# A gated layer with two weight blocks readied early and multiplied side by side, and its first halves paced 4:8

## The chip, the cores and the metric

One core of a Trainium2 chip runs the whole program in one launch. The metric is the device time of that execution in microseconds (us); lower is better. Three executions of the kernel before were timed on the chip, and one more was recorded by the hardware profiler.

## The reference

Four sequences of 448 positions pass through three layers one after the other. All inputs are float32.

```python
# attention: 4 batches x 12 heads, 448 x 64 per head
scores = cap * tanh((q @ k.T / 8) / cap)
attn = exp(scores - max); attn = attn / (sum(attn) + 1e-9)
x = attn @ v                               # [4, 448, 768]
# gated layer: 768 -> 1024 -> 768
h = maximum(x @ w_in, 0)
conv = 3-tap convolution of h along the sequence, per channel (conv_w)
x = (h * (1 / (1 + exp(-conv)))) @ w_out
# mixing: tokens (448 -> 256 -> 448), then channels (768 -> 1536 -> 768), each with a residual
u  = x + (maximum(x.T @ w_tok1, 0) @ w_tok2).T
out = u + maximum(u @ w_ch1, 0) @ w_ch2
```

## The kernel before, in words

Each operand of a product is kept as a high and a low part of a shorter type, and each product is three matmuls (`split3`: high by high, high by low, low by high). A matmul is mostly 128 x 128 weights on 128 x 448 data.

**Attention** is walked through in 96 iterations (`gi`), four to a pair of heads. An iteration multiplies scores (L146, L147), ACT makes them exponentials (L168, L169), DVE splits those into `ah` and `al` (L175, L176), and later PE multiplies them by the values (L195 to L197).

**The gated layer** of batch b is the generator `gated(b)`. Its first half has MF = 8 blocks of 18 matmuls (L466, weights `wi`). After each block ACT and DVE make one pair `gh`, `gl` out of it by Relu, convolution and gate (L470, L475 to L481); the pair of block 7 is ready last. The second half has KD = 6 blocks of 24 matmuls (L492): block m takes the weights `wo` of block m and all eight pairs, in the order k = 0 to 7, three matmuls each. So the last three matmuls of a block need pair 7. ACT takes the block's sum out of PSUM (L496), SP stores it (L497). The tiles `wo` have two buffers.

**The weights wo** are wider numbers in the input and have to be narrowed. For b = 0, `load_wo` does that in three parts of each block: 384 columns (k = 0 to 2), 384 (k = 3 to 5) and 256 (k = 6 and 7). A part is loaded by SP into `w_raw` (L352), ACT and DVE work on it in `w_pt` (L354, L357 to L359), ACT writes the high part of `wo` (L362) and DVE the low part (L366), and SP stores both to `wo_d` (L427). `w_raw` and `w_pt` have one buffer each, which other weights use too. For b over 0 a block comes back from `wo_d` by a single load of 1,024 KB (L435).

**What sets the order.** The generators are interleaved with attention by numbers of units: each `yield` says how many units the piece before it counts (W_IN in the first half, W_OUT in the second), and every iteration of attention draws 11.5 to 13 units (RATES). gated(0) to gated(2) run inside the attention of batches 1 to 3, and gated(3) beside the first steps of token mixing (L701 transposes, L718 and L732 products). Each half is 24 pieces, so the layer is 24 x 5 + 24 x 7 = 288 units. The scheduler orders each engine's instructions by priorities that follow from the place in the program; each engine, and SP's queue of DMAs, runs its own list in order.

Of the kernel before, what the change touches and what calls it, by code (L numbers as in the profile page):

```python
# [9 lines left out]
F32 = mybir.dt.float32  # L10
F32R = mybir.dt.float32r
U32 = mybir.dt.uint32
AF = mybir.ActivationFunctionType
# [4 lines left out]
B, H, S, D = 4, 12, 448, 64  # L18
NP = H // 2
DM = H * D  # L20
KD = DM // 128
DFF = 1024
MF = DFF // 128
# [7 lines left out]
QK = S + KW  # L31
YTB = 9
TKS = 100
W_IN = 5
W_OUT = 7
O_MAG = 6000
O_CAP = 0
O_SC = 0
# [35 lines left out]
def split3(whi, wlo, xhi, xlo):  # L74
    return ((whi, xhi), (whi, xlo), (wlo, xhi))
# [228 lines left out]
def fused_kernel(ctx, tc, ins, out, attention):  # L304
    nc = tc.nc
# [9 lines left out]
    ps_m = ctx.enter_context(tc.tile_pool(name="ps_m", bufs=2, space=PSUM))  # L315
# [75 lines left out]
    for _ in range(WARM):  # L391
        ps = ps_m.tile([128, 512], F32, name="mm")
# [26 lines left out]
    wo = {}  # L419

    def make_wo(m, lo, hi):

        if lo == 0:
            wo[0, m] = wo_p.tile([128, 2, MF * 128], F32R, name="wo", bufs=2)
        t = wo[0, m][:, :, lo:hi]
        narrow(st_p, 384, wide["w_out"][m, :, 2 * lo : 2 * hi], (t[:, 0], t[:, 1]))
        nc.sync.dma_start(wo_d[m, :, :, lo:hi].bitcast(F32), t.bitcast(F32))  # L427

    def load_wo(b, m):
        if b == 0:  # L430
            for lo in range(0, 1024, 384):
                make_wo(m, lo, min(1024, lo + 384))
            return
        wo[b, m] = wo_p.tile([128, 2, MF * 128], F32R, name="wo", bufs=2)
        nc.sync.dma_start(wo[b, m].bitcast(F32), wo_d[m].bitcast(F32))  # L435
# [22 lines left out]

    def gated(b):
        gs = []  # L460
        for m in range(MF):
            hi, lo = win[m]
            ps = ps_m.tile([128, 512], F32, name="mm")
            for k in range(KD):
                for n, (w, v) in enumerate(split3(hi[:, k], lo[:, k], *X[b, k])):
                    nc.tensor.matmul(ps[:, 0:S], w, v, start=k == 0 and n == 0, stop=k == KD - 1 and n == 2)  # L466
                if k % 2 and k < KD - 1:
                    yield W_IN
            h = hb[m % 2]
            nc.scalar.activation(h[:, 1 : S + 1], ps[:, 0:S], AF.Relu)  # L470
            gh = g_p.tile([128, S], F32R, name="gh", bufs=8)
            gl = g_p.tile([128, S], F32R, name="gl", bufs=8)
            gs.append((gh, gl))
            c = cv_p.tile([128, S], F32, name="c", bufs=4)
            nc.scalar.activation(c, h[:, 1 : S + 1], AF.Copy, scale=cw[:, m, 1:2])  # L475
            nc.vector.scalar_tensor_tensor(out=c, in0=h[:, 0:S], scalar=cw[:, m, 0:1], in1=c, op0=ALU.mult, op1=ALU.add)
            nc.vector.scalar_tensor_tensor(out=c, in0=h[:, 2 : S + 2], scalar=cw[:, m, 2:3], in1=c, op0=ALU.mult, op1=ALU.add)
            nc.scalar.activation(c, c, AF.Tanh, scale=0.5)
            nc.vector.scalar_tensor_tensor(out=c, in0=c, scalar=1.0, in1=h[:, 1 : S + 1], op0=ALU.add, op1=ALU.mult)
            nc.scalar.copy(gh, c)  # L480
            nc.vector.tensor_tensor(gl, c, gh.bitcast(F32), op=ALU.subtract)  # L481
            yield W_IN
        load_wo(b, 0)
        for m in range(KD):
            if m + 1 < KD:
                load_wo(b, m + 1)
            w = wo.pop((b, m)).rearrange("p t (k n) -> p t k n", n=128)
            hi, lo = w[:, 0], w[:, 1]
            ps = ps_m.tile([128, 512], F32, name="mm")
            for k in range(MF):  # L490
                for n, (w, v) in enumerate(split3(hi[:, k], lo[:, k], *gs[k])):
                    nc.tensor.matmul(ps[:, 0:S], w, v, start=k == 0 and n == 0, stop=k == MF - 1 and n == 2)  # L492
                if k % 2 and k < MF - 1:
                    yield W_OUT
            y = cv_p.tile([128, S], F32, name="c", bufs=4)
            nc.scalar.activation(y, ps[:, 0:S], AF.Copy, scale=0.5)  # L496
            nc.sync.dma_start(y_d[b, m], y)  # L497
            yield W_OUT

    def w2_early(c, i):  # L500

# [22 lines left out]
    for gi in range(NG + 3):  # L524
        g, i = divmod(gi, 4)
# [47 lines left out]
        if gi >= 24 and s3 == 4 and gi < NG:  # L573
            for p in range(NP):
                norm(b3 - 1, p, rr[b3 - 1])
            fills.append(gated(b3 - 1))
# [115 lines left out]
    def tokens(b):  # L692
# [34 lines left out]
        for m in range(KD):  # L727
# [8 lines left out]
            yield 6  # L736

    last = gated(B - 1)
    load_y(0)
    toks = [t for b in range(B - 1) for t in [tokens(b)]]  # L740
# [3 lines left out]
    n = k = 0  # L744
    begun = False
    while True:
        w = next(last, None)
# [276 lines left out]
```

## Time and profile before

| | us |
|---|---|
| median of three timed executions | 903.06 (899.55 to 904.08) |
| the profiled execution, its own time | 902.45 |
| span of that execution in the trace | 900.6 |
| PE busy | 867.5 |
| DVE busy | 696.1 |
| ACT busy | 495.5 |

The profile gives times from the start of the span; 1.85 us of the profiled execution's time lie outside it. The mean granted clock of TensorE over the span is 0.991 of full speed. The first matmul of gated(0) starts at 91.5 us and the first of its second half at 138.7 us; the second half of gated(3) has its last matmul at 522.7 us, and channel mixing takes the rest.

### The profile page before, as it was taken

The page shows a single profiled execution, that of the slowest core. Times are in us where ns is not written, and L with a number is a line of the kernel's source. Part 1 is how long each engine was busy: PE and PEld are TensorE (multiplying, and loading weights), DVE is VectorE, ACT ScalarE, POOL GpSimd, SP SyncE. Part 2 cuts the span into 40 slices and gives each one's busy share as a digit, 9 for nine tenths or more (in the row PEclk, how much of TensorE's full clock was granted, in tenths as well). Part 3 has the DMA queues.
Part 4 walks back from the last instruction along what each step waited for, and adds up shares of the span by engine and source line. Part 5 has one row for each costly group of instructions (what it writes and reads, how often), then busy time and mean ns, then how long its engine had stood idle before and what let it go on. Part 6 is the DMA issues. An engine that isn't in the chain of part 4 may idle for free.

```text
span 900.6 us, 12120 instructions
## 1 busy us (share of the span) xinstructions
PE 867.5 (96%) x4105; PEld 754.4 (84%) x4105; DVE 696.1 (77%) x1271; ACT 495.5 (55%) x820; POOL 4.7 (1%) x19
## 2 busy tenths in 40 slices
PE   8999999989989999999999998999999999999997
PEld 4665887868978889888989988789989899999996
DVE  7889987789997899956897576796967859478342
ACT  6889888767886779863764243442423423143110
POOL 0000000000000000000000000000000000000000
PEclk9999999999999999999999999999999999999999
DMA  7875564667557864457658766556473744517234
GB/s 277 268 219 171 170 201 147 208 210 243 162 177 265 283 219 145 132 181 263 219 162 258 245 199 199 157 176 195 123 245 96 224 151 126 182 55 224 76 109 140
DMA packets 81719, 168.91 MB, mean 188 GB/s; under 512 B 12050, under 2 KB 57586, under 8 KB 79346
## 3 DMA queue, kind: packets, MB, share of 16 engines
q1 hardware_dynamic: 81650, 168.07, 58.1%
q8 instruction: 34, 0.56, 0.3%
q14 instruction: 35, 0.29, 0.1%
HBM read 126.58 MB, written 38.54 MB: 183 GB/s over the span
## 4 chain that ended last, share of the span: by engine, by line
PE 54%; DVE 19%; DMA 15%; ACT 7%; issue 4%; SPq 1%; POOL 0%; DVEq 0%; ACTq 0%; POOLq 0%
PE mm L911 18%; PE o L873 14%; PE mm L492 9%; DMA w_raw<-in_w_in 3%; DMA w_raw<-in_w_out 2%; DMA c<-u_d 2%; PE mm L466 2%; PE ps_e L718 2%; PE ps_e L732 2%; DMA w_d<-w_pt 1%; DVE ab L115 1%; DMA raw<-in_qk 1%; PE ps_s L147 1%; DVE w_pt L358 1%; PE ps_s L146 1%
## 5 line engine op out<-in xcount | busy, mean ns | idle before, releaser
L911 PE MATMUL mm<-hs,w 128*128 128x448 f32 x864 | 178.4, 367 | 0.8 <-DVE rr L912 0.7
L911 PEld LDWEIGHTS mm<-hs,w 128*128 128x128 f32 x864 | 161.7, 188 | 16.2 <-DVE rr L912 1.4
L492 PE MATMUL mm<-gh,wo 128*128 128x448 f32 x384 | 127.1, 374 | 6.4 <-ACT wo L362 3.4
L466 PE MATMUL mm<-xx,wi_h 128*128 128x448 f32 x384 | 114.7, 370 | 0.2 <-DVE xx L453 0.2
L492 PEld LDWEIGHTS mm<-gh,wo 128*128 128x128 f32 x384 | 72.8, 190 | 17.2 <-ACT wo L362 5.4
L146 PE MATMUL ps_s<-ab 128*128 128x448 f32 x192 | 81.6, 426 | 2.9 <-DVE ab L115 2.1
L466 PEld LDWEIGHTS mm<-xx,wi_h 128*128 128x128 f32 x384 | 71.7, 188 | 9.2 <-issue 1.9
L168 ACT ACTIVATE a<-ps_s,icap 128x896 f32<-128x896 f32 x76 | 67.0, 885 | 22.4 <-PE ps_s L147 17.9
L492 PE MATMUL mm<-gl,wo 128*128 128x448 f32 x192 | 71.2, 371 | 0.4 <-DVE gl L481 0.4
L147 PE MATMUL ps_s<-low,ab 128*128 128x448 f32 x192 | 71.3, 373 | 0.3 <-DVE low L116 0.3
L169 ACT ACTIVATE a<-a,cap 128x896 f32<-128x896 f32 x76 | 70.4, 926 | 1.3
L466 PE MATMUL mm<-xx,wi_l 128*128 128x448 f32 x192 | 70.3, 366 | 0.0
L176 DVE TENSOR_TENSOR al<-a,ah 128x896 fp32r<-128x896 f32 (+1 forms) x56 | 54.3, 971 | 1.7
L873 PE MATMUL o<-u,wi_h 128*128 128x448 f32 x216 | 49.4, 363 | 1.4 <-ACT u L790 1.1
L790 ACT CAST u<-c 128x448 fp32r<-128x448 f32 x48 | 27.0, 567 | 42.5 <-DVE c L798 21.9
L873 PE MATMUL o<-u,wi_l 128*128 128x448 f32 x216 | 47.9, 362 | 0.0
L146 PEld LDWEIGHTS ps_s<-ab 128*128 128x128 f32 x192 | 36.3, 190 | 13.4 <-issue 5.0
L175 DVE CAST ah<-a 128x896 fp32r<-128x896 f32 (+1 forms) x56 | 31.5, 565 | 18.9 <-PE ob L196 9.6
L873 PEld LDWEIGHTS o<-u,wi_h 128*128 128x128 f32 x216 | 40.5, 188 | 5.1 <-ACT u L790 1.9
L147 PEld LDWEIGHTS ps_s<-low,ab 128*128 128x128 f32 x192 | 36.4, 190 | 9.0 <-issue 5.4
L873 PEld LDWEIGHTS o<-u,wi_l 128*128 128x128 f32 x216 | 40.5, 187 | 2.7
L111 ACT CAST ab<-raw 128x960 fp32r<-128x960 f32 x36 | 35.4, 992 | 12.3 <-DMA raw<-in_qk 7.1
(166 smaller groups left out, 1690.5 us busy)
## 6 DMA issues: line engine op xcount, KB each, us to landing
wo<-wo_d SPq DMA_DIRECT2D x18, 1024.0 KB
raw<-in_qk SPq DMA_DIRECT2D x18, 960.0 KB
w_raw<-in_w_ch SPq DMA_DIRECT2D x40, 384.0 KB
c<-u_d SPq DMA_DIRECT2D x60, 224.0 KB
w_raw<-in_w_in SPq DMA_DIRECT2D x16, 384.0 KB
e<-in_qk SPq DMA_DIRECT2D x6, 960.0 KB
y_d<-c SPq DMA_DIRECT2D x24, 224.0 KB
yt<-y_d SPq DMA_DIRECT2D x24, 224.0 KB
```

The lines of the kernel that those rows point to most:

```text
L111: nc.scalar.copy(h, r)
L146: nc.tensor.matmul(ps[:, bank, 0:S], a[:, keys], a[:, 0:S], start=start, stop=False)
L147: nc.tensor.matmul(ps[:, bank, 0:S], a[:, keys], low, start=False, stop=stop)
L168: nc.scalar.activation(a[:, 0:n], ps[:, 0:n, 0:S], AF.Tanh, scale=self.c["icap"])
L169: nc.scalar.activation(a[:, 0:n], a[:, 0:n], AF.Exp, scale=self.c["cap"])
L175: nc.vector.tensor_copy(ah[:, 0:n], a[:, 0:n])
L176: nc.vector.tensor_tensor(al[:, 0:n], a[:, 0:n], ah[:, 0:n].bitcast(F32), op=ALU.subtract)
L466: nc.tensor.matmul(ps[:, 0:S], w, v, start=k == 0 and n == 0, stop=k == KD - 1 and n == 2)
L492: nc.tensor.matmul(ps[:, 0:S], w, v, start=k == 0 and n == 0, stop=k == MF - 1 and n == 2)
L790: nc.scalar.copy(w[:, 0], t)
L873: nc.tensor.matmul(ps, l, r, start=k == 0 and n == 0, stop=k == 2 and n == 2)
L911: nc.tensor.matmul(ps[:, 0:S], l, x, start=r == 0 and n == 0, stop=r == 3 and n == 2)
```

## The change

The pieces of gated(0) count 4 units in the first half and 8 in the second in place of 5 and 7 (the sum stays 288); those of the other layers keep 5 and 7. The weights of blocks 0 and 1 are asked for ahead of the blocks m = 5 and m = 7 of the first half, not at its end; those of block m + 2 when block m is done. For b over 0 the second half multiplies block 0 up to k = 6, then block 1 up to k = 6, then k = 7 of block 0 and of block 1, and then blocks 2 to 5 whole. For b = 0 the blocks keep their order.

```diff
-W_IN = 5
-W_OUT = 7
+PACE = (4, 8), (5, 7)
+WO_AT = 5, 7
...
     def gated(b):
         gs = []
+        w_in, w_out = PACE[b > 0]
         for m in range(MF):
+            if m in WO_AT:
+                load_wo(b, WO_AT.index(m))
...
-            yield W_IN
-        load_wo(b, 0)
-        for m in range(KD):
-            if m + 1 < KD:
-                load_wo(b, m + 1)
-            w = wo.pop((b, m)).rearrange("p t (k n) -> p t k n", n=128)
-            hi, lo = w[:, 0], w[:, 1]
-            ps = ps_m.tile([128, 512], F32, name="mm")
-            for k in range(MF):
-                for n, (w, v) in enumerate(split3(hi[:, k], lo[:, k], *gs[k])):
-                    nc.tensor.matmul(ps[:, 0:S], w, v, start=k == 0 and n == 0, stop=k == MF - 1 and n == 2)
-                if k % 2 and k < MF - 1:
-                    yield W_OUT
+            yield w_in
+        acc = {}
+
+        def mm(m, k):
+            if k == 0:
+                acc[m] = ps_m.tile([128, 512], F32, name="mm")
+            w = wo[b, m].rearrange("p t (k n) -> p t k n", n=128)
+            for n, (l, v) in enumerate(split3(w[:, 0, k], w[:, 1, k], *gs[k])):
+                nc.tensor.matmul(acc[m][:, 0:S], l, v, start=k == 0 and n == 0, stop=k == MF - 1 and n == 2)
+
+        def done(m):
+            del wo[b, m]
             y = cv_p.tile([128, S], F32, name="c", bufs=4)
-            nc.scalar.activation(y, ps[:, 0:S], AF.Copy, scale=0.5)
+            nc.scalar.activation(y, acc.pop(m)[:, 0:S], AF.Copy, scale=0.5)
             nc.sync.dma_start(y_d[b, m], y)
-            yield W_OUT
+            if m + 2 < KD:
+                load_wo(b, m + 2)
+
+
+        blocks = [[(0, k) for k in range(MF - 1)] + [(1, k) for k in range(MF - 1)] + [(0, MF - 1), (1, MF - 1)]] if b else [[(m, k) for k in range(MF)] for m in range(2)]
+        blocks += [[(m, k) for k in range(MF)] for m in range(2, KD)]
+        n = 0
+        for m, k in (i for l in blocks for i in l):
+            mm(m, k)
+            if k == MF - 1:
+                done(m)
+            n += 1
+            if n % 2 == 0:
+                yield w_out
```

Line numbers move with it: L466 becomes L469, L475 to L481 become L478 to L484, L492 becomes L493, L496 and L497 become L498 and L499, and every line from L504 on moves by 15.

**First place.** DVE in the first layer, at the `al` of the head whose values PE multiplies at 145.81 us in the trace of before. Before (`c`, `gl` and `h1` are the gate's tiles, `w_pt` the weights being narrowed, `low`, `ab` and `v2` the splitting of queries, keys and values):

```order
L175 CAST ah_1365<-a_1362 128x896 [waits Activation_49]
L476 SCALAR_TENSOR_TENSOR c_1253<-h1_179,cw_94,c_1253 128x448 [waits Activation_49]
L357 TENSOR_SCALAR w_pt_1384<-w_pt_1384 128x384 [waits Activation_49]
L477 SCALAR_TENSOR_TENSOR c_1253<-h1_179,cw_94,c_1253 128x448 [waits DVE_49]
L115 TENSOR_TENSOR ab_1462<-raw_1369,ab_1462 64x512 [waits Activation_49]
L116 TENSOR_TENSOR low_1463<-raw_1369,ab_1462 128x448
L479 SCALAR_TENSOR_TENSOR c_1253<-c_1253,h1_179 128x448 [waits Activation_49]
L358 SCALAR_TENSOR_TENSOR w_pt_1384<-w_raw_1383,w_pt_1384 128x384 [waits DMAHW4_49,DVE_49]
L136 TENSOR_TENSOR v2_1471<-vs_1472,v1_1467 128x512 [waits DMAHW0_49,Activation_49]
L359 SCALAR_TENSOR_TENSOR w_pt_1384<-w_pt_1384 128x384 [waits DVE_49]
L481 TENSOR_TENSOR gl_1252<-c_1253,gh_1251 128x448 [waits Activation_49]
L176 TENSOR_TENSOR al_1366<-a_1362,ah_1365 128x896
```

And now:

```order
L482 SCALAR_TENSOR_TENSOR c_1271<-c_1271,h1_179 128x448 [waits Activation_49]
L175 CAST ah_1418<-a_1415 128x896 [waits Activation_49]
L484 TENSOR_TENSOR gl_1270<-c_1271,gh_1269 128x448 [waits Activation_49]
L176 TENSOR_TENSOR al_1419<-a_1415,ah_1418 128x896 [waits DVE_49]
L357 TENSOR_SCALAR w_pt_1353<-w_pt_1353 128x384 [waits Activation_49]
L115 TENSOR_TENSOR ab_1515<-raw_1422,ab_1515 64x512 [waits Activation_49]
L358 SCALAR_TENSOR_TENSOR w_pt_1353<-w_raw_1352,w_pt_1353 128x384 [waits DMAHW4_49,DVE_49]
```

Between `ah` and the `al` that goes with it stood ten instructions, among them three of narrowing and four of the gate; now one of the gate stands there.

**Second place.** PE in the first layer, in the last block of its second half (number 5), at the last of its weights' three parts (k = 6 and 7). Before, with the end of the 16 rows (18 matmuls) of the next layer's first block that stand between k = 5 and k = 6:

```order
L466 MATMUL mm_2019<-xx_1985,wi_h0_241 128x448 [waits Activation_49]
L466 MATMUL mm_2019<-xx_1985,wi_h0_241 128x448
L466 MATMUL mm_2019<-xx_1985,wi_l0_242 128x448
L466 MATMUL mm_2019<-xx_1991,wi_h0_241 128x448 [waits Activation_49]
L466 MATMUL mm_2019<-xx_1991,wi_h0_241 128x448 [waits DVE_49]
L466 MATMUL mm_2019<-xx_1991,wi_l0_242 128x448
L466 MATMUL mm_2019<-xx_1997,wi_h0_241 128x448 [waits Activation_49]
L466 MATMUL mm_2019<-xx_1997,wi_h0_241 128x448 [waits DVE_49]
L466 MATMUL mm_2019<-xx_1997,wi_l0_242 128x448
L492 MATMUL mm_1878<-gh_1179,wo_1750 128x448 [waits Activation_49]
L492 MATMUL mm_1878<-gl_1180,wo_1750 128x448
L492 MATMUL mm_1878<-gh_1179,wo_1750 128x448 [waits DVE_49]
```

Now, from k = 5 on:

```order
L493 MATMUL mm_1871<-gh_1056,wo_1714 128x448
L493 MATMUL mm_1871<-gh_1137,wo_1714 128x448
L493 MATMUL mm_1871<-gl_1138,wo_1714 128x448
L493 MATMUL mm_1871<-gh_1137,wo_1714 128x448
L451 MATMUL mm_1994<-rr_1924,sel_177 128x448 [waits DVE_49]
L493 MATMUL mm_1871<-gh_1185,wo_1714 128x448 [waits Activation_49]
L493 MATMUL mm_1871<-gl_1186,wo_1714 128x448
L493 MATMUL mm_1871<-gh_1185,wo_1714 128x448 [waits DVE_49]
L493 MATMUL mm_1871<-gh_1269,wo_1714 128x448
L493 MATMUL mm_1871<-gl_1270,wo_1714 128x448
L493 MATMUL mm_1871<-gh_1269,wo_1714 128x448
L469 MATMUL mm_2019<-xx_1967,wi_h0_241 128x448 [waits DVE_49]
```

The next layer's first block (now L469) has moved behind the whole of block 5. From the first matmul of k = 3 of this block to the first of k = 6 there are 13 rows of PE now; between them no row of the next layer is left.

**Third place.** PE in the second layer, at the last pair. Before, in block 0 (`mm_2527`):

```order
L492 MATMUL mm_2527<-gh_2427,wo_2523 128x448 [waits Activation_49]
L492 MATMUL mm_2527<-gl_2428,wo_2523 128x448 [waits DVE_49]
L195 MATMUL oa_2707<-ah_2592,v1_1235 128x448
L492 MATMUL mm_2527<-gh_2427,wo_2523 128x448
L196 MATMUL oa_2707<-ah_2592,v2_2510 64x448
L197 MATMUL oa_2707<-al_2593,v1_1235 128x448 [waits DVE_49]
L492 MATMUL mm_2527<-gh_2483,wo_2523 128x448 [waits Activation_49]
L195 MATMUL oa_2707<-ah_2592,v1_1235 128x448
L196 MATMUL oa_2707<-ah_2592,v2_2510 64x448
L197 MATMUL oa_2707<-al_2593,v1_1235 128x448
L146 MATMUL ps_s_2714<-ab_2505 128x448 [waits PE_49]
L147 MATMUL ps_s_2714<-low_2506,ab_2505 128x448
```

Now block 0 is `mm_2527` and block 1 is `mm_2578`, whose k = 0 to 6 stands ahead of k = 7 of block 0:

```order
L197 MATMUL ob_2730<-al_2679,v1_1333 128x448 [waits DVE_49]
L493 MATMUL mm_2527<-gh_2487,wo_2326 128x448 [waits Activation_49]
L195 MATMUL ob_2730<-ah_2678,v1_1333 128x448
L493 MATMUL mm_2527<-gl_2488,wo_2326 128x448
L196 MATMUL ob_2730<-ah_2678,v2_2514 64x448
L493 MATMUL mm_2527<-gh_2487,wo_2326 128x448
L197 MATMUL ob_2730<-al_2679,v1_1333 128x448
L493 MATMUL mm_2578<-gh_2487,wo_2458 128x448
L493 MATMUL mm_2578<-gl_2488,wo_2458 128x448
L493 MATMUL mm_2578<-gh_2487,wo_2458 128x448
L146 MATMUL ps_s_2795<-ab_2636 128x448 [waits PE_49,Activation_49]
L147 MATMUL ps_s_2795<-low_2637,ab_2636 128x448
```

The pairs 6 and 7 began six rows apart in block 0; now the other block's k = 0 to 6 stands between them, and pair 7 is first used 44 rows later in PE's list. On DVE eight instructions stood between the `ah` and the `al` of the head multiplied here (`al_2593` before); now one does. Block 2 begins 26 rows behind the last row of block 0, and its first row is the one that waits for a DMA, the load of its weights. The same place of the last layer on SP, where that load (`wo_4783`) is issued, now:

```order
L750 DMA u_d_81<-yt_4180 128x448 [waits DVE_49]
L750 DMA u_d_81<-yt_4183 128x448 [waits DMAHW0_49,DVE_49]
L499 DMA y_d_80<-c_4780 128x448 [waits Activation_49]
L435 DMA wo_4783<-wo_d_79 128x2048 [waits DMAHW2_49,PE_49]
L703 DMA yt_4684<-y_d_80 128x448 [waits DMAHW7_49]
L704 DMA yt_4684<-y_d_80 128x64
L703 DMA yt_4687<-y_d_80 128x448 [waits DMAHW5_49,DMAHW0_49]
```

In before, the load of the block behind block 0 stood ahead of the store of block 0 (L497); now it stands behind this store and behind two stores of `u_d`, which wait for DVE.

## Rows read from the trace of the kernel before

**Rows 1.** Page, part 1: busy us, share of the span, instructions

```profile
PE 867.5 (96%) x4105; PEld 754.4 (84%) x4105; DVE 696.1 (77%) x1271; ACT 495.5 (55%) x820; POOL 4.7 (1%) x19
```

**Rows 2.** Windows: stretch, then busy us (count) per engine, clock, DMA

```profile
150.00:175.00 25.00, 25.00 (x124) 22.31 (x123) 18.35 (x34) 17.84 (x29) 0.00 (x0) 0.99 0.53 177
175.00:200.00 25.00, 20.83 (x89) 16.52 (x88) 22.42 (x38) 18.13 (x28) 0.63 (x1) 0.93 0.61 198
```

**Rows 3.** Waits of PE, 138 to 220 us: total us, times, longest

```profile
PE mm L492 <- ACT wo L362: 3.4, 3, 1.4
```

**Rows 4.** PE, timeline of first layer: start, us, instruction, [idle before <-releaser]

```profile
145.81 0.47 PE L197 MATMUL oa<-al,v 128*128 128x448 f32 x1 [2.10 <-DVE al L176]
...
179.36 0.47 PE L492 MATMUL mm<-gh,wo 128*128 128x448 f32 x1 [1.38 <-ACT wo L362]
...
212.02 0.47 PE L492 MATMUL mm<-gh,wo 128*128 128x448 f32 x1 [1.01 <-ACT wo L362]
...
218.42 0.47 PE L492 MATMUL mm<-gh,wo 128*128 128x448 f32 x1
```

**Rows 5.** Windows of 2.5 us behind four of the stops (clock third from last)

```profile
145.00:147.50 2.50, 1.69 (x7) 1.51 (x8) 2.39 (x3) 1.61 (x2) 0.00 (x0) 0.91 1.02 413
147.50:150.00 2.50, 2.50 (x8) 2.20 (x8) 1.85 (x3) 2.00 (x4) 0.00 (x0) 0.50 0.30 116
150.00:152.50 2.50, 2.50 (x13) 2.12 (x12) 2.02 (x4) 1.96 (x5) 0.00 (x0) 0.91 0.48 173
180.00:182.50 2.50, 2.20 (x9) 1.84 (x9) 2.10 (x4) 1.67 (x4) 0.00 (x0) 0.73 0.77 221
182.50:185.00 2.50, 2.50 (x9) 2.04 (x8) 2.22 (x6) 2.28 (x5) 0.00 (x0) 0.58 1.00 356
212.50:215.00 2.50, 2.50 (x12) 1.76 (x12) 2.29 (x5) 0.93 (x2) 0.00 (x0) 1.00 0.71 265
270.00:272.50 2.50, 2.50 (x7) 2.16 (x8) 2.50 (x5) 0.86 (x1) 0.00 (x0) 0.50 1.00 340
272.50:275.00 2.50, 2.50 (x12) 2.19 (x11) 1.31 (x2) 1.38 (x3) 0.00 (x0) 0.84 0.31 57
```

**Rows 6.** DVE, timeline ahead of the stop before 145.81

```profile
138.61 0.63 DVE L175 CAST ah<-a 128x896 fp32r<-128x896 f32 x1 [0.95 <-ACT a L169]
...
144.68 1.08 DVE L176 TENSOR_TENSOR al<-a,ah 128x896 fp32r<-128x896 f32 x1
```

**Rows 7.** PE, timeline of the second and third layer

```profile
268.42 0.47 PE L197 MATMUL oa<-al,v 128*128 128x448 f32 x1 [1.42 <-DVE al L176]
269.97 0.74 PE L492 MATMUL mm<-gh,wo 128*128 128x448 f32 x1 [1.08 <-ACT gh L480]
...
382.53 0.47 PE L492 MATMUL mm<-gl,wo 128*128 128x448 f32 x1 [0.40 <-DVE gl L481]
```

**Rows 8.** ACT, timeline: last block's weights being narrowed

```profile
204.69 0.51 ACT L362 CAST wo<-w_pt 128x384 fp32r<-128x384 f32 x1
...
211.47 0.51 ACT L362 CAST wo<-w_pt 128x384 fp32r<-128x384 f32 x1
...
217.97 0.41 ACT L362 CAST wo<-w_pt 128x256 fp32r<-128x256 f32 x1 [2.41 <-DVE w_pt L359]
```

**Rows 9.** SP issues, a PE wait, and a window, around two reloads

```profile
273.61 0.33 SPq L435 DMA_DIRECT2D wo<-wo_d  x1
274.19 0.32 SPq L497 DMA_DIRECT2D y_d<-c  x1
...
410.76 0.32 SPq L435 DMA_DIRECT2D wo<-wo_d  x1
...
416.66 0.44 PE L492 MATMUL mm<-gh,wo 128*128 128x448 f32 x1 [0.98 <-DMA wo<-wo_d]
...
276.00:278.00 2.00, 2.00 (x12) 1.84 (x11) 1.96 (x5) 1.00 (x3) 0.00 (x0) 1.00 0.97 401
```

More of the change, by code (lines that the diff above doesn't have):

```diff
@@ L481, in gated @@
             nc.vector.tensor_tensor(gl, c, gh.bitcast(F32), op=ALU.subtract)
-            yield W_IN
-        load_wo(b, 0)
-        for m in range(KD):
-            if m + 1 < KD:
-                load_wo(b, m + 1)
-            w = wo.pop((b, m)).rearrange("p t (k n) -> p t k n", n=128)
-            hi, lo = w[:, 0], w[:, 1]
-            ps = ps_m.tile([128, 512], F32, name="mm")
-            for k in range(MF):
-                for n, (w, v) in enumerate(split3(hi[:, k], lo[:, k], *gs[k])):
-                    nc.tensor.matmul(ps[:, 0:S], w, v, start=k == 0 and n == 0, stop=k == MF - 1 and n == 2)
-                if k % 2 and k < MF - 1:
-                    yield W_OUT
+            yield w_in
+        acc = {}
[7 more added lines that the diff above has]
+            del wo[b, m]
             y = cv_p.tile([128, S], F32, name="c", bufs=4)
-            nc.scalar.activation(y, ps[:, 0:S], AF.Copy, scale=0.5)
+            nc.scalar.activation(y, acc.pop(m)[:, 0:S], AF.Copy, scale=0.5)
             nc.sync.dma_start(y_d[b, m], y)
-            yield W_OUT
+            if m + 2 < KD:
[10 more added lines that the diff above has]
+                yield w_out
     def w2_early(c, i):
```

## The prediction

> **What bounds the kernel now.** I went from the page to stretches, from stretches to waits, and from waits to single instructions. The page has PE busy for 867.5 of 900.6 us [rows 1]; the next engine, DVE, has 77%. So the end is set by PE's list, and a change that removes no matmul can win only the time in which PE stands still or runs at a lower granted clock. The change removes no matmul: it reorders them. PE's order differs from before only between about 88 us and about 505 us; behind that the lists agree row by row. So whatever happens must happen in the four gated layers.
>
> At full clock PE goes through a matmul in 0.20 us: 150 to 175 us has 124 of them in 25.00 us without idle time [rows 2]. In that unit I count cover below. PE's waits in the first layer name weights still being narrowed: three waits of the second half's matmuls for ACT's high part, 3.4 us in all [rows 3]. The timeline gives the single stops: 2.10 us at 145.81 for an `al`, 1.38 us at 179.36 and 1.01 us at 212.02 for `wo` [rows 4]; the third wait of [rows 3] is the remaining 1.01. Then comes a price that the waits don't show. Behind the 145.81 stop the granted clock is 0.91, 0.50 and 0.91 in three windows of 2.5 us [rows 5]; 0.50 is the 1.2 GHz level, the rest mixes it with 2.4 GHz. What is lost is 2.5 x (0.09 + 0.50 + 0.09) = 1.7 us. Behind 179.36: 0.73 and 0.58, 2.5 x (0.27 + 0.42) = 1.7 us. Behind the stops at 268 to 270 us: 0.50 and 0.84, 1.7 us. Behind the 1.01 us stop at 212.02 it stays at 1.00 [rows 5]. So a stop of 1.4 us can cost twice itself, and one of 1.0 us only itself.
>
> **Part by part.** All against the profiled run's 902.45 us, which is 0.6 us under the median of the runs, 903.06.
>
> *The `al` stop of the first layer: -3.8.* DVE began the `ah` at 138.61 and the `al` that belongs to it at 144.68, 6.07 us later [rows 6]: ten instructions of narrowing, gate and splitting lay between. The first place shows one left. Half a microsecond each, the nine that go give 5 us, over twice the 2.10 us stop; besides, block 1's first matmuls now stand on PE ahead of it. I take the stop and its clock away: 2.1 + 1.7 = 3.8.
>
> *The waits for narrowed weights: -1.6 for 179.36, 0 for the others.* With 4:8 the first half yields more often per unit, so more of PE's matmuls, ACT's and DVE's gate work move ahead, and with loads at m = 5 and 7 the narrowing begins earlier. But it remains a chain through one `w_raw` and one `w_pt`: the parts of the last block come 6.78 us (204.69 to 211.47) and 6.50 us (to 217.97) apart [rows 8], whatever PE wants. Counting order rows at the stop of 179.36 (block 3, last part), PE has 1.4 us less work ahead of it and ACT and DVE some 2.8 us less, so the weights gain 1.4 us on it: just the size of the stop. That leaves it anywhere between whole and gone with its clock, 0 to -(1.38 + 1.7) = -3.1; I take half, -1.6. The same count gives about 0 at the 1.01 us stops, and I leave them, with +-2 for both together.
>
> *The last block's third part: +2.0.* In before PE reached k = 3 of block 5 at 212.02 and k = 6 at 218.42, without a wait there, 6.40 us apart [rows 4], which is the pace of the chain. What filled those 6.40 us was mainly the first 18 matmuls of the next layer. In the second place they have moved behind: 13 matmuls, 2.6 us, are left between. If the parts still come 6.50 us apart, PE waits 3.9 us; if the chain is faster by all it has, nothing. ACT's L362 sat idle 2.41 us there [rows 8] on DVE's three steps, among DVE work that is now partly elsewhere, so some is won back. I take the middle, +2.0; a fall of the clock would add 1.7.
>
> *The last pair in layers two to four: -4.6.* Before 268.42 PE waited 1.42 us for an `al`, right after it 1.08 us for `gh` of pair 7, then ran at 0.50; at 382.53 it waited 0.40 us for `gl` [rows 7]. In the third place pair 7 is used 44 rows later (44 x 0.20 = 8.8 us of matmuls), and seven DVE instructions of about half a microsecond have left the space ahead of the `al`, 3.5 us against 1.42. All goes: 1.42 + 1.08 + 1.7 + 0.40 = 4.6.
>
> *What pays for it: the loads of block 2, +4.5.* In before a block's buffer was reloaded while the other whole block was multiplied. Now blocks 0 and 1 end together, so block 2's load goes out with little behind it. From the issue at 410.76 to the use at 416.66 a 1,024 KB load took 5.9 us, and PE had waited 0.98 us for it [rows 9]; that is the upper bound. The lower: at the 401 GB/s of 276 to 278 us, right behind another such load, its bytes alone take 2.6 us [rows 9].
> Second layer: from block 0's last matmul to block 2's first are 26 rows, 5.2 us; the issue comes about half a microsecond behind the matmul's start, so 4.7 us are left. Wait between 0 and 1.2; I take 1.0, nearer to the row of a real landing.
> Third layer: same cover, but on SP a store (L521) that waits for DVE work some 12 matmuls, 2.4 us, further on stands ahead of the load. 0 to 3.6; I take half, 1.8.
> Fourth layer: the cover is 36 rows (L747 and others), 7.2 us, but the load stands behind two stores of `u_d` that wait for DVE and behind `y_d`'s, which waits for ACT; issues are 0.58 us apart (273.61, 274.19 [rows 9]), so three are 1.7 us, and the evacuation is another half. 7.2 - 0.5 - 1.7 - 0.5 = 4.5: a wait of 0 to 1.4 without DVE being late, more if it is. I take 1.7.
> Together 0 to about 8, +4.5 as taken, and each could bring a clock fall of 1.7.
> On this path the Trainium skill has a figure: "DMA: Bandwidth & Descriptors", "Anatomy of one DMA", fits 2.0 us plus the bytes at 436 GB/s for GpSimd's path. An estimate by that page for these loads is 4.4 us, by which the second layer would wait nothing and the sum would be about 3 us lower; the row of 5.9 us says otherwise, though it may have had other transfers ahead of it.
>
> *The sum:* -3.8 - 1.6 - 4.6 + 2.0 + 4.5 = -3.5, so 902.45 - 3.5 = 898.95, and with the 0.6 us to the median 899.5. The `yield`s themselves cost nothing: they set only the order, and the pieces after about 505 us stand as before.
>
> **The rivals.**
> *Loads hidden, weights in time (0.22).* Block 2's loads land like the bare bytes, 2.6 us, under 4.5 us or more of cover, and the stop of 179.36 goes whole: -3.8 - 3.1 - 4.6 + 2.0 = -9.5, 893.5. For it: the lower bounds are as good as the upper ones, and the DMA engines are busy only 0.53 of a quiet stretch [rows 2]. Against: 5.9 us is the one landing that PE's wait shows.
> *The narrowing chain sets the pace anyway (0.20).* PE comes earlier and waits for the same parts: the 179.36 stop stays with its clock, and the last block costs the whole 3.9 and 1.7 more: -3.8 - 4.6 + 5.6 + 4.5 = +1.7, 904.8 at the median. For it: 6.5 us a part, one buffer. Against: the chain's own engines get 2.8 us of relief.
> *Slower: block 2's loads late in three layers (0.08).* Each is held behind other transfers by some 4 us and PE's clock falls behind each: 3 x (4 + 1.7) = 17.1 in place of 4.5, so -8.0 + 17.1 = +9.1, 912. It decides from 12.5 us on for the three together (-8.0 + 12.5 = +4.5). For it: three 384 KB loads in front, 1.2 MB at 401 GB/s, make 2.9 us, and the 5.9 us row already has a wait. Against: 4 us would be a landing of about 8.7 us.
>
> **How the numbers follow.** My forecast has 0.50, with a range of its own of 896 to 903. A measurement here tells about 0.5% from no change, 4.5 us, which is also the spread of the three runs. Faster is below 898.5: two fifths of the forecast's half (0.20) and nearly all of the first rival (0.21), 0.41. Slower is above 907.6: the third rival (0.08), a sixth of the second (0.03) and a remnant of the forecast (0.01), 0.12. Same is the rest, 0.47. The range 892.5 to 907 leaves out the third rival and the outer parts of the other two.
>
> **What would show it.** In the profile after: no stop of PE at the first layer's first `al`, and none for pair 7 behind 260 us, with the granted clock near 1.00 there; PE waiting for ACT's `wo` at k = 6 of the first layer's last block by 0 to 3.9 us; and three waits for `wo<-wo_d` at block 2 of layers two to four. PE's idle time in 88 to 505 us plus clock loss should be 3 to 4 us lower. The prediction is wrong if new stops of over 1.4 us lower the clock at places that I count as covered, or if the loads land in 3 us.

## The result, and the profile after

The changed kernel takes 913.45 us, median of six (907.71 to 914.71), against 901.53 for the kernel before on the same chip (899.55 to 904.77): ratio 1.0107, interval 1.0078 to 1.0136. It is slower by 1.1%, outside the range of 892.5 to 907. The profiled execution took 914.06 us, 11.6 more than that of before.

The page's first part, to be held against [rows 1]:

```profile
PE 872.9 (96%) x4105; PEld 755.4 (83%) x4105; DVE 695.0 (76%) x1271; ACT 494.7 (54%) x820; POOL 3.9 (0%) x19
```

The share of PE is the same 96%, and PE idles 39.0 us of the span in place of 33.1; the rest of the difference stands in its busy time, in which the ends of matmuls are modelled. To see where the time goes I number PE's matmuls, 0 to 4104 in both, and read when the n-th starts. (That is worked out from the two traces; it needs no matching of instructions.)

```
n-th matmul        300   480    600    840   1080   1440   1860   2280   4104
before, us        94.0 134.80 164.16 223.38 276.67 351.01 439.45 519.10 894.32
after - before    +0.5  +0.9   -2.6   +1.9   -0.7   +5.0   +8.7  +12.9  +11.4
```

Between 480 and 600 lies the first layer's `al` stop, up to 840 the rest of that layer, up to 1440 the second, to 1860 the third and to 2280 the fourth; each of these stretches reaches into the first half of the layer that follows. So 3.5 us are won at the `al`, 4.5 lost behind it; 2.6 won at the second layer's last pair, 5.6 lost behind it; then 3.8 and 4.2 lost, and nothing of note in channel mixing.

PE's waits from 88 to 510 us of the changed kernel (total, times, longest):

```profile
PE mm L493 <- ACT wo L362: 5.7, 4, 2.5
PE mm L493 <- DMA wo<-wo_d: 5.7, 4, 2.2
PE ob L195 <- DVE ah L175: 1.9, 1, 1.9
PE ps_e L733 <- DVE xx L720: 1.9, 1, 1.9
PE mm L451 <- DVE xx L453: 1.8, 2, 1.6
PE ps_s L146 <- ACT a L168: 1.3, 1, 1.3
```

The waits for `wo` from ACT have gone from 3.4 [rows 3] to 5.7 us, those for reloads from one of 0.98 [rows 9] to four with 5.7. PE's timeline of the first layer, the places of [rows 4]:

```profile
147.80 0.37 PE L197 MATMUL oa<-al,v 128*128 128x448 f32 x1
...
181.04 0.47 PE L493 MATMUL mm<-gh,wo 128*128 128x448 f32 x1 [2.51 <-ACT wo L362]
...
196.56 0.47 PE L195 MATMUL ob<-ah,v 128*128 128x448 f32 x1 [1.95 <-DVE ah L175]
...
208.94 0.47 PE L451 MATMUL mm<-rr,sel 128*128 128x448 f32 x1 [1.59 <-DVE xx L453]
...
214.70 0.47 PE L493 MATMUL mm<-gh,wo 128*128 128x448 f32 x1 [1.17 <-ACT wo L362]
```

The first `al` is there without a wait (147.80), as forecast. But PE now meets the weights at the beginning of blocks 4 and 5 (2.51, and 1.66 at 202.20) and at the last part of block 5 (1.17), and waits for an `ah` and for an `xx` of the next layer. The later layers:

```profile
272.05 0.47 PE L195 MATMUL oa<-ah,v 128*128 128x448 f32 x1 [1.25 <-DVE ah L175]
...
294.85 0.47 PE L493 MATMUL mm<-gh,wo 128*128 128x448 f32 x1 [1.75 <-DMA wo<-wo_d]
...
403.26 0.47 PE L493 MATMUL mm<-gh,wo 128*128 128x448 f32 x1 [0.49 <-DMA wo<-wo_d]
...
419.01 0.44 PE L493 MATMUL mm<-gh,wo 128*128 128x448 f32 x1 [2.21 <-DMA wo<-wo_d]
...
467.82 0.68 PE L733 MATMUL ps_e<-xx,wt 128*128 128x384 f32 x2 [1.92 <-DVE xx L720]
...
496.19 0.47 PE L493 MATMUL mm<-gh,wo 128*128 128x448 f32 x1 [1.20 <-DMA wo<-wo_d]
```

At 268 to 270 us the stops of [rows 7] are gone; a new one of 1.25 for an `ah` stands beside their place. The reload waits are at block 3 of layer two (294.85), blocks 2 and 4 of layer three (403.26, 419.01) and block 2 of layer four (496.19). The one at 467.82 is for token mixing's `xx`. Windows behind five of these stops, clock third from last, as in [rows 5]:

```profile
182.50:185.00 2.50, 2.50 (x9) 2.20 (x8) 1.53 (x3) 1.39 (x2) 0.00 (x0) 0.51 1.02 403
197.50:200.00 2.50, 2.49 (x13) 1.88 (x12) 1.90 (x4) 2.00 (x4) 0.00 (x0) 1.00 0.76 200
272.50:275.00 2.50, 2.38 (x13) 1.77 (x11) 2.40 (x4) 1.03 (x2) 0.00 (x0) 1.00 0.83 215
420.00:422.50 2.50, 2.50 (x10) 2.20 (x9) 2.44 (x4) 0.02 (x1) 0.00 (x0) 0.59 0.84 329
470.00:472.50 2.50, 2.50 (x11) 2.41 (x11) 2.24 (x5) 1.64 (x5) 0.00 (x0) 0.67 0.00 0
```

The clock falls to the 1.2 GHz level behind 181.04, 419.01 and 467.82 and not behind 196.56 or 272.05. All clock lost from 88 to 505 us, summed over 2.5 us windows below 0.97, is 5.1 us in both kernels, three falls of 1.7 us each, so on balance the clock costs nothing. PE's idle time in this stretch is 14.0 us before (417 us less 403.0 of busy time) and 23.0 us now (417 less 394.0), where the prediction had idle time and clock loss together 3 to 4 us lower. So of the 12.4 us lost between matmuls 300 and 2280 some 9 are waiting that the trace shows as idle time; the other 3 us or so show neither as idle time nor as clock.

### The profile page after: what moved, and what is told of

The parts are those of the page before. It is cut to its first block, busy times and chain, and to the rows that moved or that the text cites. A ratio compares the mean times of both kernels' runs of the same rounds, so it can differ in the third digit from the quotient of the medians.

```text
span 911.9 us, 12125 instructions
## 1 busy us (share of the span) xinstructions
PE 872.9 (96%) x4105; PEld 755.4 (83%) x4105; DVE 695.0 (76%) x1271; ACT 494.7 (54%) x820; POOL 3.9 (0%) x19
## 4 chain that ended last, share of the span: by engine, by line
PE 47%; DVE 20%; DMA 19%; ACT 9%; issue 4%; SPq 1%; ACTq 0%; DVEq 0%
PE o L888 11%; PE mm L926 11%; PE mm L493 7%; DMA w_raw<-in_w_out 4%; DMA c<-u_d 3%; PE mm L469 3%; DMA wo<-wo_d 3%; PE ps_e L733 2%; PE oa L191 2%; PE ob L191 2%; PE ps_s L146 2%; DMA w_raw<-in_w_tok 2%; PE ps_s L147 2%; DMA raw<-in_qk 2%; PE ps_e L747 1%
## 5 line engine op out<-in xcount | busy, mean ns | idle before, releaser
L493 PE MATMUL mm<-gh,wo 128*128 128x448 f32 x384 | 128.3, 380 | 12.2 <-ACT wo L362 5.7
L469 PE MATMUL mm<-xx,wi_h 128*128 128x448 f32 x384 | 113.9, 369 | 0.2 <-DVE xx L453 0.2
L493 PEld LDWEIGHTS mm<-gh,wo 128*128 128x128 f32 x384 | 73.5, 192 | 23.7 <-ACT wo L362 7.5
L469 PEld LDWEIGHTS mm<-xx,wi_h 128*128 128x128 f32 x384 | 71.8, 188 | 8.9 <-issue 1.3
L493 PE MATMUL mm<-gl,wo 128*128 128x448 f32 x192 | 72.1, 376 | 0.2 <-DVE gl L484 0.2
L469 PE MATMUL mm<-xx,wi_l 128*128 128x448 f32 x192 | 70.7, 368 | 0.0
L175 DVE CAST ah<-a 128x896 fp32r<-128x896 f32 (+1 forms) x56 | 31.4, 563 | 13.6 <-PE ob L196 6.8
L493 PEld LDWEIGHTS mm<-gl,wo 128*128 128x128 f32 x192 | 37.0, 193 | 4.2 <-DVE gl L484 0.5
```

Of the source, the lines that this page charges most:

```text
L175: nc.vector.tensor_copy(ah[:, 0:n], a[:, 0:n])
L493: nc.tensor.matmul(acc[m][:, 0:S], l, v, start=k == 0 and n == 0, stop=k == MF - 1 and n == 2)
```

## The experiments

All numbers are ratios to the kernel before, run beside it on the same chip, with a 95% interval. "Woven" means blocks 0 and 1 side by side up to k = 6. "Ahead of" and "behind the yield" is where the reload of block m + 2 is asked for: in `done(m)`, as in the changed kernel, or after the `yield` that follows, which is where before had it. The four columns are what each kernel's one profiled execution gained (-) or lost (+) in us against that of before in each layer, by the n-th matmul (300 to 840, to 1440, to 1860, to 2280).

```
              ratio  interval          first second third fourth
changed      1.0107 1.0078 to 1.0136   +1.4  +3.0   +3.8  +4.2
e1_first     1.0035 0.9996 to 1.0073   +1.3  -2.4   -0.6  +0.3
e2_later     1.0122 1.0053 to 1.0191   +2.4  +3.1   +1.7  +3.0
e3_pace      1.0018 0.9978 to 1.0058   -3.0  +2.4   +0.1  -0.4
e5_noweave   1.0045 1.0008 to 1.0081   +1.2  -0.6   +4.0  -0.2
e6_noload    1.0088 1.0056 to 1.0120   +3.2  +5.5   -0.6  +1.9
e7_loadfirst 1.0110 1.0068 to 1.0152   +2.4  +1.0   +6.2  +2.1
e8_stagger   1.0082 1.0052 to 1.0111   +2.3  -0.5   +4.3  -0.2
e9_move      1.0028 0.9998 to 1.0058   +3.5  +0.8   -0.1  +3.7
f1_weave     1.0059 1.0024 to 1.0095   -2.3  +0.6   +2.0  +6.5
f2_early     0.9982 0.9952 to 1.0012   -2.9  +1.1   +2.3  -0.0
f3_mini      1.0038 1.0013 to 1.0063   -1.5  -0.7   +4.3  +0.8
f4_minipace  1.0046 1.0017 to 1.0075   -2.2  -1.7   +5.0  +3.5
g1_second    0.9994 0.9972 to 1.0016   +0.0  +1.5   +1.6  -0.8
g2_last      1.0048 1.0010 to 1.0086   +1.4  -0.4   +0.8  +6.4
g3_third     1.0072 1.0046 to 1.0099   +1.3  +2.6   +6.2  +0.1
```

**Which half of the change?** Against the changed kernel, e1 keeps only the first layer's part, e2 only that of the later layers, e5 takes back the weave:

```diff
 e1_first, against the changed kernel
-            if m in WO_AT:
+            if b == 0 and m in WO_AT:
-... (1, MF - 1)]] if b else [[(m, k) ...
+... (1, MF - 1)]] if False else [[(m, k) ...
 e2_later
-PACE = (4, 8), (5, 7)
+PACE = (5, 7), (5, 7)
-            if m in WO_AT:
+            if b > 0 and m in WO_AT:
 e5_noweave
-... (1, MF - 1)]] if b else [[(m, k) ...
+... (1, MF - 1)]] if False else [[(m, k) ...
 e3_pace, against before: W_IN, W_OUT = PACE[b > 0] in gated(b)
```

Where the early loads are off, blocks 0 and 1 are asked for at before's places. In e1, e2 and e5 the reloads stay in `done(m)`, ahead of the `yield`, in all four layers, also in those that the expectations call as before.

> The first layer as in the changed kernel (4:8, early loads, its block order), layers two to four as before: loads at the end of the first half, blocks one after the other. Theory A (the loss comes mostly from the woven blocks 0 and 1 and the loads behind them in layers two to four; by the offset of the two traces the first layer gives only +1 of the +12 us): 0 to +3 us against before. Theory B (the first layer's narrowing chain, met earlier by PE, is the loss and the rest is a shift that follows from it): +6 to +12 us.

> Layers two to four as in the changed kernel, the first layer's pace and loads as before. Theory A: +7 to +11 us against before, with PE waits for wo<-wo_d at block 2 or 3 of the three layers. Theory B: under +3 us.

> The changed kernel with one part undone: in layers two to four blocks 0 and 1 are multiplied one after the other again; the early loads and 4:8 stay. Theory A with the weave as its cause: +0 to +4 us against before, no wait for wo<-wo_d over 1 us in layers two and three. Rival (the early loads, which stand in SP's queue ahead of other transfers, are the cause, not the weave): +7 us or more, as the changed kernel.

> The kernel before with the pace of the first layer alone changed to 4:8. If the pace by itself is harmless (theory A): -2 to +2 us. If the pace makes PE meet the narrowing chain too early (theory B): +3 us or more, with waits for ACT's wo grown from 3.4 us to 6 or more.

e2 has the whole loss (1.0122), e1, e3 and e5 less than half of it or none: theory A, and theory B falls: the larger part lies in the later layers, and with the weave gone more than half of the loss is gone. But e2 also has the first layer's reloads ahead of the `yield` (+2.4 us there), 0.45% stay in e5, and its reload wait in layer three (3.6 us at block 5, without any weave) is over the expectation's bound.

**Is it the reloads behind the weave?** In e6 they are left out, in e7 they stand ahead of the stores, in e8 the weave is cut short:

```diff
 e6_noload, in done(m), against the changed kernel
-                load_wo(b, m + 2)
+                if b:
+                    wo[b, m + 2] = w
+                else:
+                    load_wo(b, m + 2)
 e7_loadfirst, in done(m), ahead of the evacuation
+            if b and m + 2 < KD:
+                load_wo(b, m + 2)
 e8_stagger
-[(1, k) for k in range(MF - 1)] + [(0, MF - 1), (1, MF - 1)]
+[(1, k) for k in range(3)] + [(0, MF - 1)] + [(1, k) for k in range(3, MF)]
 e9_move, against before: the reload of block m + 2 in done(m), nothing else
```

> The changed kernel, in layers two to four with blocks 2 to 5 multiplied by the weights that blocks 0 and 1 have left in their buffers, so that their reloads are left out (the output is another one). Theory A1 (the woven blocks end together, both buffers come free at once, and PE meets the reloads of blocks 2 to 4): the four waits for wo<-wo_d, 5.7 us, go, and with what follows from them 6 to 9 us: about 905 us, within 4 us of before. Theory A2 (the weave costs by its order of PE's rows, in waits for attention's and token mixing's ACT and DVE steps): under 3 us back, 910 us or more.

> The changed kernel with each reload of layers two to four written ahead of the evacuation and the store of the block that frees the buffer, so that block 3's load no longer stands behind two stores of y_d on SP. If SP's order is the larger part of A1: the 1.75 us wait in layer two goes and the others shrink, 3 to 5 us back against the changed kernel. If the missing cover is: 0 to 2 us back, the loads of blocks 2 and 3 then run into each other.

> The changed kernel with the weave cut short in layers two to four: block 0 up to k = 6, block 1 up to k = 2, block 0's k = 7, then the rest of block 1. Blocks 0 and 1 end 15 matmuls apart and 9 matmuls still stand ahead of the last pair. Theory A1: reload waits fall from 5.7 to under 2.5 us, the time comes back by 5 to 8 us, 905 to 908 us. Theory A2: half of the weave's order is left, 2 to 4 us back.

> The kernel before with one thing changed: the weights of block m + 2 are asked for when block m is done, ahead of the yield, not at the start of block m + 1. Theory: no change, -2 to +2 us. Rival (the call's earlier place alone reorders the narrowing in the first layer and makes the 4 us that two other kernels lost between 164 and 223 us): +3 to +5 us by 223 us, and waits for ACT's wo of over 4.5 us in place of 3.4.

e6 came back by 0.2% only, which by its expectation speaks for A2. Its trace, one execution, says more. In layers three and four, 4.4 and 2.3 us come back against the changed kernel, as A1 has it. In layer two a new stop, of the next layer's first matmul for `rr`, takes the place of the reload's; PE's row and a window behind it:

```profile
322.03 0.71 PE L451 MATMUL mm<-rr,sel 128*128 128x448 f32 x1 [5.83 <-DVE rr L446]
...
322.50:325.00 2.50, 2.50 (x8) 2.20 (x8) 1.21 (x3) 1.02 (x2) 0.00 (x0) 0.50 0.03 11
```

That one stop (5.83 us and three windows near 0.5) hides what the reloads gave back. So the columns speak for A1 in layers three and four, and layer two's price in e6 is of another kind; what delays `rr` there was not followed. e7: the 1.75 us wait in layer two went, but those of layers three and four grew to 5.4 us together, and the time is the changed kernel's: SP's order is not the larger part. e8 gave back 0.25%, the size that A2 expects, and had a reload wait of 3.93 us at 421 us: still a loss. e9 shows that the place of the call matters in the first layer by +3.5 us, but its ratio alone is within noise.

**The weave alone, the call alone, the layers one by one.** All of these have the reload behind the yield:

```diff
 in all seven
-            if m + 2 < KD:
-                load_wo(b, m + 2)
+            if m + 2 < KD:
+                pend.append(m + 2)
...
                 yield w_out
+                while pend:
+                    load_wo(b, pend.pop(0))
 f1_weave:    PACE (5, 7) twice; early loads off
 f2_early:    early loads for b == 0 alone; weave off
 f3_mini:     as f1, but the weave of e8
 f4_minipace: as f3, with PACE (4, 8), (5, 7); early loads off as in f3
 g1_second:   as f2, woven if b == 1
 g2_last:     as f1, woven if b == 3
 g3_third:    as f1, woven if b == 2
```

> The weave alone: the kernel before with only blocks 0 and 1 of layers two to four woven up to k = 6; all loads are asked for at before's places (the reload behind the yield), pace 5:7. Theory W (the weave is the loss, by reload waits and the stops that follow in layers two to four): the first layer as before up to 250 us, then +6 to +9 us. Rival M (the moved calls for the loads are the loss, in all four layers): 0 to +3 us.

> First layer with 4:8 and its blocks 0 and 1 asked for at m = 5 and 7, but reloads asked for behind the yield as in before; no weave, layers two to four as before. If the call ahead of the yield is what lost 4 us between 164 and 223 us: -3 to -1 us at 223 us against before, as with the pace alone (-2.4). If asking at m = 5 and 7 is: +1 to +3 us there.

> The kernel before with three contractions (9 matmuls) of block 1 put ahead of block 0's last pair in layers two to four, nothing else. Theory W: the stop of 1.42 + 1.08 us and its clock in layer two goes (-2.6 as in the changed kernel) and blocks 0 and 1 still end 15 matmuls apart, so that reload waits stay at 1 to 2 us in all: -4 to 0 us. If any weave upsets the later layers: +2 to +5 us.

> The same three contractions, and 4:8 with early loads in the first layer, reloads asked for behind the yield everywhere. If the parts add up (first layer -2.4, second -2.6, nothing lost): -6 to -2 us, the fastest so far. If gains of single stops are eaten by later ones: -1 to +3 us.

f1: the weave alone costs 0.59%, theory W. f2: with the call behind the yield, 4:8 and the early loads are harmless. The weave alone (0.59%) and the changed kernel without it (e5, 0.45%) together make 1.04%, about the whole 1.07%. f4's expectation speaks of early loads, but its edit has none: it is f3 with the pace 4:8. f3 and f4 missed: with three contractions 3.11 us and 2.66 us are lost at a reload in layer three, which eats what the second layer gives. Not all of that need be the weave's: f2 and e5, unwoven, wait 1.97 and 3.60 us at a reload there, before 0.98.

> 4:8 and early loads in the first layer, reloads asked for behind the yield, and the weave in layer two alone. If the weave is good where the last pair was late and its losses lie in layers three and four: the second layer's stop goes (-2.3 to -2.6 us) on top of the first layer's -2, -2 to -5 us against before. If the weave loses in layer two as well (reload waits, then the next layer's first rows): -1 to +2 us.

> The kernel before with the weave in the last layer alone. If the 5 us that the weave alone lost behind 363 us lie mostly in the last layer, in token mixing's rows between 450 and 500 us: +3 to +5 us, with waits for L726's xx of over 2 us; else under +2 us.

> The kernel before with the weave in the third layer alone. If its loss is the reload of blocks 2 and 4 (2.4 us more than before in the weave alone): +1 to +3 us, waits for wo<-wo_d at blocks 2 and 4; else 0 to +1 us, or a gain of 0.4 us, the stop of pair 7 there.

g1 is no gain and no loss: in layer two the weave earns nothing net. g2 and g3 lose 0.48% and 0.72%; g3's 6.5 us are more than it was expected to lose, and the two together more than f1, which is woven in both layers, so what a single layer costs is not settled by these ratios. g3's rows of PE at the reloads of blocks 2 and 4, and windows behind them:

```profile
403.73 0.47 PE L497 MATMUL mm<-gh,wo 128*128 128x448 f32 x1 [1.22 <-DMA wo<-wo_d]
...
420.90 0.44 PE L497 MATMUL mm<-gh,wo 128*128 128x448 f32 x1 [2.08 <-DMA wo<-wo_d]
...
405.00:407.50 2.50, 2.50 (x9) 2.25 (x8) 0.15 (x1) 0.00 (x0) 0.00 (x0) 0.51 0.84 305
422.50:425.00 2.50, 2.50 (x8) 2.20 (x8) 2.50 (x3) 0.00 (x0) 0.00 (x0) 0.50 0.93 311
```

These are two stops of 3.3 us and two falls of the clock, and blocks 2 and 4 are the ones expected. Part of g2's time goes at token mixing's rows. PE of g2 (L753 is L732, L722 is L701, L739 is L718 of before):

```profile
485.98 0.36 PE L753 MATMUL ps_e<-wt,hl 128*128 128x448 f32 x1
486.19 0.82 PE L722 MATMUL ps_d<-ident,yt 128*128 128x128 f32 x6
487.25 0.61 PE L739 MATMUL ps_e<-xx,wt 128*128 128x384 f32 x2 [0.24 <-ACT xx L724]
489.93 0.33 PE L722 MATMUL ps_d<-ident,yt 128*128 128x128 f32 x1 [2.07 <-DVE xx L726]
```

and of before, at the same transposes:

```profile
486.72 0.57 PE L492 MATMUL mm<-gh,wo 128*128 128x448 f32 x2
487.32 1.01 PE L701 MATMUL ps_d<-ident,yt 128*128 128x128 f32 x6
488.09 0.45 PE L492 MATMUL mm<-gl,wo 128*128 128x448 f32 x1
488.37 0.37 PE L492 MATMUL mm<-gh,wo 128*128 128x448 f32 x1
```

In before the matmuls of L492 stand between the transposes and the rows that need their result, and cover ACT's and DVE's step between them. They are block 2's. In g2 block 1 ends at the same place of PE's list as in before (matmul 2052), but block 0, whose buffer block 2 needs, ends 61 matmuls later, and block 2 begins at matmul 2103 instead of 2065. SP issues the load of block 2's weights at 465.38 in before and at 487.88 in g2, where it stands behind the stores of blocks 0 and 1 and two stores of `u_d`:

```profile
465.38 0.33 SPq L435 DMA_DIRECT2D wo<-wo_d  x1
```

```profile
486.08 1.71 SPq L756 DMA_DIRECT2D u_d<-yt  x2
487.88 0.38 SPq L435 DMA_DIRECT2D wo<-wo_d  x1
```

So in g2 the transposes follow each other bare, PE waits 2.07 us for an `xx`, and the clock falls behind it (1.7 us). The wait for `c` at the fourth layer's first contractions, 1.21 us at 460 us in before, is 2.70 us in g2; but that lies ahead of the first row of PE that the weave moves (matmul 1986), so this difference is not shown to be the weave's.

## Why the prediction was wrong, by its own steps

By the stretches of the first table the `al` stop gave -3.5 us where I had -3.8, the rest of the first layer +4.5 for +0.4, the last pair -2.6 for -4.6, and what follows it in layers two to four +13.6 for the loads' +4.5. So the two terms that failed are the narrowed weights in the first layer and everything that the weave pays behind the last pair.

**The `al` stop of the first layer, -3.8: right, with luck in its size.** Measured -3.5 between matmuls 480 and 600, and -2.8 to -3.9 in all ten kernels with 4:8, the pace alone included. But 1.7 of the 3.8 is a fall of the clock that the same stop need not bring. f1 has before's lists up to here and the same stop of 2.10 us, at 146.20, and its clock stays at 1.00, where before has 0.50 [rows 5]:

```profile
147.50:150.00 2.50, 2.50 (x14) 2.23 (x14) 1.84 (x3) 2.50 (x5) 0.00 (x0) 1.00 0.50 195
```

Before and the four kernels with its lists here (f1, f3, g2, g3) lie between -1.5 and +0.2 at this place, -0.7 in the mean; against that mean the change is worth 2.8 us.

**The waits for narrowed weights, -1.6, and the last block's third part, +2.0: together +0.4, measured +4.5. This step failed.** The last part was about right, 1.17 us and no fall of the clock. What I missed is the first parts of blocks 4 and 5 (2.51 and 1.66 us) and two stops of attention and of the next layer (1.95, 1.59). I counted the work ahead of PE, ACT and DVE at the stops of before, and took it that the `yield`s cost nothing; but on which side of the `yield` a reload is asked for moves the narrowing itself, and the attention rows with it. Six kernels with 4:8 and the call ahead of the yield lost 1.2 to 3.2 us in the first layer (mean +2.0), four with 4:8 and the call behind it -3.0 to 0.0 (mean -2.0). Without 4:8 it is +2.4 and +3.5 against a mean of -0.2 over five. f2, which has everything else of the first layer's change, still waits for `wo` as long, 6.0 us:

```profile
PE mm L497 <- ACT wo L362: 6.0, 6, 1.6
```

but not for `ah` or `xx`, and its clock doesn't fall there. e1 and f2 differ by the side of this call alone, in all layers: +1.3 and -2.9 us in the first layer, 1.0035 and 0.9982 in time. So that the call costs 3 to 4 us is shown; which of the narrowing's instructions pushes the attention rows back was not followed further.

**The last pair, -4.6: right in mechanism, too large.** No stop for pair 7 is left in layers two to four, and the clock of 272.5 to 275 us is 1.00 against 0.84 [rows 5]. But a new wait of 1.25 us for attention's `ah` stands at the same place: -2.6 between matmuls 840 and 1080, where the prediction has -4.2 (its 0.40 lies in layer three). Here too 1.7 is the clock: e1, without the weave, still waits 1.47 us for pair 7, at full clock, and gains 2.7.

**The loads, +4.5: the sum right by luck, the places and the time of a load wrong, and the terms behind it left out.** Reload waits grew by 4.7 us. For layers two, three and four I took 1.0, 1.8 and 1.7 at block 2; block 2 waits 0, 0.49 and 1.20, and the two largest waits (1.75, 2.21) are at blocks 3 and 4, where I had none. SP's rows in layers two and three show why:

```profile
280.67 0.32 SPq L435 DMA_DIRECT2D wo<-wo_d  x1
285.28 0.32 SPq L521 DMA_DIRECT2D w_d<-w_pt  x1
285.70 0.37 SPq L519 DMA_DIRECT2D w_raw<-in_w_ch  x1
286.16 0.87 SPq L499 DMA_DIRECT2D y_d<-c  x2
287.09 0.51 SPq L435 DMA_DIRECT2D wo<-wo_d  x1
...
411.12 0.38 SPq L435 DMA_DIRECT2D wo<-wo_d  x1
```

Block 2's load went out at 280.67, right behind block 0's last matmul. Block 1's last came 0.8 us later, but block 3's load stands behind a store of `w_d` that waits for DVE until 285.28, a load of `w_raw` and two stores of `y_d` (which ACT had ready by 283.3), and went out at 287.09; PE used it at 294.85. (In e7, where it stands ahead of the `y_d` stores, layer two has no reload wait.) In layer three the load issued at 411.12 was used at 419.01. That is 7.8 and 7.9 us from issue to use, over my upper bound of 5.9, which a single transfer had given. The Trainium skill's figure that I quoted, 4.4 us by "DMA: Bandwidth & Descriptors", "Anatomy of one DMA", is further off still for a load amid others; the uncontended case is not shown apart here.

**What the prediction left out altogether** is that the cover was borrowed. I counted the 26 to 36 rows behind the woven blocks as free cover for the reload; in before block 2 began 10 to 13 rows behind block 1's last, and its matmuls stood among those rows and covered ACT's and DVE's steps. Now block 2 comes 22 to 33 rows behind, and 51 in g2, where the bare rows cost 2.07 us and a fall of the clock. In the changed kernel itself the stops inside these rows are small, 0.36 us at 284.84 and 0.34 at 494.37. Its two other large stops lie elsewhere. At 340.68 PE waits 1.26 us for an `a`: 11 rows of PE lie between the attention scores there and the ones ahead of them, 22 in before. At 467.82 PE's rows are those of before (the lists agree from matmul 1680 to 1985), but DVE makes the `xx` later, behind channel mixing's weights (`ba`) and not ahead of them, in before and now:

```profile
454.59 0.55 DVE L705 TENSOR_TENSOR xx<-ps_d,xx 128x384 fp32r<-128x384 f32 x1
...
456.92 0.55 DVE L345 SCALAR_TENSOR_TENSOR ba<-w_pt,ba 128x384 uint32<-128x384 uint32 x1
```

```profile
466.74 0.55 DVE L345 SCALAR_TENSOR_TENSOR ba<-w_pt,ba 128x384 uint32<-128x384 uint32 x1
467.21 0.55 DVE L720 TENSOR_TENSOR xx<-ps_d,xx 128x384 fp32r<-128x384 f32 x1
```

g3, woven in layer three alone, has this order too and waits 0.84 us there: the weave reorders other engines' lists well behind itself. Of the 13.6 us lost behind the two gains (5.6, 3.8 and 4.2), stops of over 0.3 us make 6.5, with the 4.7 of the reloads in them, and the falls behind 419.01 and 467.82 make 3.4; the rest, 3.7 us, shows in no such stop. The two falls, at places that I counted as covered, are the prediction's own sign of being wrong.

By the table's columns the weave costs, as the mean of the five executions with it in full against the eight without it (before counted, e6 and the short weaves left out), 1.8 against 0.4 us in layer two, 4.0 against 1.0 in layer three, 4.4 against 0.3 in layer four: 8.5 us together. The eight spread from -2.4 to +2.6 in layer two, so its share is not clear of that. In f1, which has the weave alone, the executions lost 0.59%, 5.3 us, which is the firmer number.

**The rivals.** The slower one named the right mechanism's first half (late loads in three layers, 912 us) and its time was the nearest, but not its size: reload waits of 5.7, not 12, us with one fall of the clock, not three. I gave it 0.08, since I let it come about only by loads that land late, and none of my cases had waits that spread to attention and token mixing. The range fell short for the same reason.

No version beat before clearly: f2 (0.9982, interval up to 1.0012) and g1 (0.9994) can't be told from it. A third buffer for `wo`, by which a reload would not have to wait for the end of the weave, was not tried.

## What to carry to other kernels

Work that is put ahead to cover one wait is taken from behind another: before counting rows as cover for a transfer, look at what stood among those rows and covered them, and read the waits of the next layer's steps too. Blocks that end together free their buffers together, and their reloads then stand in one queue, behind each other and behind the stores of both. Where a scheduler orders by place in the program, the side of a `yield` on which work is asked for is a change of its own, and is worth a run of its own.

## What the runs showed of the hardware that was not expected

Executions with the same instructions in the same order differ by several microseconds in the first layer. Before, f1, f3, g2 and g3 have the same lists up to about 240 us, and the n-th matmul count gives 0, -2.3, -1.5, +1.4 and +1.3 us there. PE's waits for narrowed weights in f1, and then in g2, from 138 to 223 us:

```profile
PE mm L497 <- ACT wo L362: 2.4, 3, 1.5
```

```profile
PE mm L497 <- ACT wo L362: 6.1, 4, 2.9
```

Before has 3.4 us [rows 3]. So a difference of 2 us in one layer between two profiles says nothing by itself; I read mine only where several kernels agree.

A stop's length does not decide whether the clock falls: behind 1.95 us at 196.56 it stayed at 1.00, behind 1.38 us in before it fell to 0.58 [rows 4, 5], and the `al` stop of 2.10 us brought a fall in before and none in f1. So a clock term read from one execution is a chance, not a price.
